# Batch 0's k and q loaded by landmark windows, with sums before the turn, in a Nystrom attention and MLP kernel on one core

## The chip, the cores and the metric

One core of a Trainium2 chip. The metric is the time on the device in microseconds (us) of one run of the kernel. TensorE (PE; its weight loads stand apart as PEld) does matrix products, VectorE (DVE) and ScalarE (ACT) the elementwise work and reductions, GpSimd (POOL) some elementwise work and DMA issues, SyncE (SP) issues most DMAs.

## The reference

Nystrom attention over 4 batches, 8 heads, 576 tokens and 64 dimensions, and two MLPs after it. The landmarks are means over windows of 18 tokens:

```python
q_lm = q.reshape(B, H, 32, 18, D).mean(axis=3)
k_lm = k.reshape(B, H, 32, 18, D).mean(axis=3)
A, Bm, C = sm(q, k_lm), sm(q_lm, k_lm), sm(q_lm, k)
Z = Bm.T / (norm1(Bm) * norminf(Bm) + 1e-6)
for _ in range(6):
    Z = 2 * Z - Z @ Bm @ Z
x = A @ Z @ C @ v
h = x @ w_in
x = (max(h, 0) + alpha * min(h, 0)) @ w_out
h = x @ w_in2
out = (h * clip(h + 3, 0, 6) / 6) @ w_out2
```

`sm` is a softmax of the scaled products. q and k have factor 8 on their draw. x is put as 2304 rows of 512 ahead of the MLPs. The MLP weights w_in, w_out, w_in2 and w_out2 come in 64-bit floats and are decoded on the chip to 32-bit.

## The kernel before, in words

Constants: P = 128 partitions, M = 32 landmarks a head, W = 18 tokens a landmark, HS = 288 (half the tokens), NF = 4 full tiles of 128 tokens and a tail of 64 tokens, NP = 4 pairs of heads, NG = 2 heads in a pair. A head h is 2 j + g.

The kernel is one long program. Batch 0's attention is the head of it: nothing of the MLP can start without it. Then the first MLP runs in 16 items for each of two blocks of tokens in each batch (`Block1`, L807 and L836: item n computes one 128-row piece of h, then adds its product with w_out). The attention of the next batch runs beside the blocks as background work, in steps. The second MLP follows at the end.

In the head (L763 to L786) the order on TensorE, VectorE, ScalarE and SP is the order of the program, written out by hand; in the blocks that holds for TensorE and SP, and a scheduler at compile time puts the others in order. Where TensorE would wait, `warm(n)` (L764) issues n idle matmuls of 512 columns; eight open the program.

Batch 0, `attention(0, ..., lat=0)`:

- `load_long` (L251): the tail of 64 tokens with tokens on partitions, and the other 512 tokens with 4 consecutive tokens of a head on a partition, for k and q in four parts of two heads each. So 5 DMAs for each of k and q, all on SP; then alpha, v in 2 DMAs, and the weights w_in and w_out.
- `transposed_long` (L294): turns k, then q, to 64 dimensions x 2 heads on the partitions and tokens in the row (kT, qT). The tail takes 4 transposes (L299); each pair of heads takes 8 matmuls with the identity (L307), each of which the profile shows as two instructions. ScalarE copies from PSUM (L300, L311) and VectorE then sums each 18 tokens of the copy to a landmark (L312). POOL copies k's landmarks into a block diagonal form `bdk` (L337), which was set to zero at the start (L153).
- `compared` (L354): products of q's landmarks with kT and with k's landmarks, for both halves of the tokens and g (L359). Then maxima on VectorE, exponentials on ScalarE (`exp_b`, `exp_c`), then `blocks`, `turned_c` (C turned, L477), `norms` (L405), `turned_rest` (L483) and `product` with v (L494).
- `scores` (L428) of tiles 0 and 1: q against k's landmarks, with bdk as moving operand (L435). Their products stand beside the softmax, their maximum ahead of the inverse and the rest inside it.
- `inverse` (L503): six steps, each a set of 8 small products (L510), then VectorE and ScalarE work. A list `fill` puts between the steps what else is to be done: a number n stands for n pieces of weight decoding (`early`, on ScalarE; `joins` brings VectorE's part), a0, n0 and t0 for steps of scores, normalisation and turning of tiles 0 and 1. A piece of w_in is two ScalarE operations on 256 columns (L202, L210) and one VectorE operation (L217); a piece of w_out has one on ScalarE (L202, 512 columns), one on POOL (L206) and one on VectorE.
- Then `project` (L698) multiplies the result with w_in's first columns, and the blocks begin. The scores of tiles 2 to 4 (a list `rest`) run in batch 0's first items.

In the blocks, item n first decodes weights up to a level that depends on how many pieces `early` did in the head (`emitted`, `LEAD`): `LEAD = max(2, emitted[0] + 1)`, where emitted[0] counts w_out pieces.

Of the kernel before, what the change touches and what calls it, by code (L numbers as in the profile page):

```python
# [64 lines left out]
def kernel(  # L65
# [28 lines left out]
    P = 128  # L94
# [15 lines left out]
    NC = FF // 512  # L110
    wide = w_in.dtype not in (F32,)
# [41 lines left out]
    nc.gpsimd.memset(bdk, 0.0)  # L153

# [96 lines left out]
    def load_long(src, b, nm, parts=1, home=None):  # L251

        if home is None:
            raw = sb.tile([P, NTI * H * D], F32, tag="raw", name=nm, bufs=2)
            home = raw[:, :NF * H * D], raw[:, NF * H * D:]
        full = home[0].rearrange("p (h c) -> p h c", h=H)
        tail = home[1][:TAIL].rearrange("p (h d) -> p h d", h=H)
        nc.sync.dma_start(out=tail, in_=src[b, :, FULL:, :].rearrange("h p d -> p h d"))
        for i in range(parts):
            hs = slice(i * H // parts, (i + 1) * H // parts)  # L260
            nc.sync.dma_start(out=full[:, hs], in_=src[b, hs, :FULL, :].rearrange("h (p t) d -> p h (t d)", t=NF))
        return full, tail

    def attention(b, bank, lat, early=None, joins=None, rest=None, warm=lambda n: None, consts=None):
# [29 lines left out]
        def transposed_long(raw, xt, lm):  # L294

            full, tail = raw
            ps = bank("tp").rearrange("q (j p) -> q j p", j=NP)
            for j in range(NP):
                nc.tensor.transpose(ps[:, j, :TAIL], tail[:, NG * j:NG * j + NG, :], ident[:TAIL, :TAIL])  # L299
            nc.scalar.copy(xt[:, :, FULL:S], ps[:, :, :TAIL])  # L300
            warm(1)
            yield True
            for j in range(NP):
                ps = bank("tp")
                for t in range(NF):
                    for g in range(NG):
                        nc.tensor.matmul(  # L307
                            ps[64 * g:64 * g + 64, t:FULL:NF], lhsT=full[:, NG * j + g, t * D:(t + 1) * D], rhs=ident,
                            start=True, stop=True,
                        )  # L310
                nc.scalar.copy(xt[:, j, :FULL], ps)  # L311
                nc.vector.tensor_reduce(  # L312
                    out=lm[:, j], in_=xt[:, j, :S].rearrange("p (l r) -> p l r", r=W), op=ALU.add, axis=AX.X
                )
                yield True

        if not lat:
            raws["k", b] = load_long(k, b, "rk", NP)
# [4 lines left out]
        qlm = small([NP, M], "qlm")  # L323
        rq = load(q, b, "rq") if lat else load_long(q, b, "rq", NP)
        turn = transposed if lat else transposed_long
# [5 lines left out]
        for _ in turn(raws["k", b], kT, kT[:, :, S:]):  # L331
            yield True
        if lat:
            rv, rv_rest = load_long(v, b, "rv")
        for g in range(NG):
            gp = slice(64 * g, 64 * g + 64)
            nc.gpsimd.tensor_copy(bdk[gp, :, g], kT[gp, :, S:])  # L337
        yield True
        for _ in turn(rq, qT, qlm):
            yield True  # L340
# [13 lines left out]
        def compared(g, hf):  # L354
            lo, hi = ((0, HS), (HS, S + M))[hf]
            ps = scs[g, hf] = bank("sc")
            for j in range(NP):
# [70 lines left out]
        def scores(tiles):  # L428
# [3 lines left out]
            for t in tiles:  # L432
                o = ps[:n, (t - t0) * 2 * P:(t - t0 + 1) * 2 * P].rearrange("p (g j l) -> p g j l", g=NG, j=NP)
                for j in range(NP):
                    nc.tensor.matmul(o[:, :, j], lhsT=qT[:, j, t * P:t * P + n], rhs=bdk[:, j], start=True, stop=True)  # L435
# [22 lines left out]
        def turned(tiles):  # L458
# [3 lines left out]
            for g in range(NG):  # L462
                for t in tiles:
                    c = (t - t0) * P
                    nc.tensor.transpose(ps[:, g, c:c + sizes[t]], es[:sizes[t], t, g], ident[:sizes[t], :sizes[t]])
# [6 lines left out]
        def turned_c(g, copy=nc.scalar.copy):  # L472
# [3 lines left out]
            for t in range(NF):  # L476
                nc.tensor.transpose(ps[:, t], pcs[:, g, t:FULL:NF], ident)  # L477
            copy(cts[0][:, g, :NF], ps)

        def turned_rest():  # L480
            ps = bank("ctp").rearrange("p (g c) -> p g c", g=NG)
            for g in range(NG):
                nc.tensor.transpose(ps[:TAIL, g, :P], pcs[:, g, FULL:], ident)  # L483
# [19 lines left out]
        def inverse():  # L503
            x = x0
            for it in range(6):
# [7 lines left out]
                if it == 5:  # L513
                    r6, vd = small([NG, P], "r6"), small([NG, D], "vd")
                    rs6 = small([NG, M], "rs6")
# [42 lines left out]
        if not lat:  # L558

            for hf in (1, 0):  # L560
                for g in range(NG):
# [6 lines left out]
            for g in range(NG):  # L568
# [9 lines left out]
            turned_rest()  # L578
            c_scale()
            drain(product())  # L580
            consts()
            warm(6)
            next(a0)
            early(1)
            n0, t0 = normalised([0, 1]), turned([0, 1])
            early(1)
            joins(1)
            fill = [[2, a0], [2, 1], [2, n0], [1, n0], [2, 1], [t0, 1], [1]]
            for i, _ in enumerate(inverse()):
# [6 lines left out]
                warm((5, 5, 4, 4, 3, 3, 6)[i])  # L596
# [166 lines left out]
    with tc.manual_schedule(engines=set(first)):  # L763
# [8 lines left out]
        warm(8)  # L772
# [492 lines left out]
```

## Time and profile before

| what | value |
|---|---|
| median of 3 runs | 810.71 us (810.41 to 810.74) |
| the profiled execution's own time | 808.85 us |
| its span in the profile | 807.0 us |
| instructions | 16974 |
| PE busy | 789.3 us (98%) |
| PEld busy | 734.3 us (91%) |
| DVE busy | 588.2 us (73%) |
| ACT busy | 455.4 us (56%) |
| POOL busy | 215.2 us (27%) |

The profile is of one execution on the chip. A busy TensorE in it is not TensorE at its peak: matmuls are pipelined and their ends are modelled, so that a matmul that is short of data can look long. The chain of waits is followed back from the last instruction: at each step to what released it, or to the instruction before it on its engine; "issue" is time in which the engine waited for nothing that the profile shows. An arrow reads as "output <- inputs", and 128x512 is partitions by elements.

### The profile page before, as it was taken

The numbers are of one execution on the slowest core, as the hardware profiler recorded it, in microseconds if no ns is written. First come the engines' busy times: TensorE is split into PE (matmuls) and PEld (weight loads), VectorE is DVE, ScalarE is ACT, GpSimd is POOL, SyncE is SP. The second block draws the span as 40 slices with busy tenths as digits, with TensorE's granted clock in tenths as the row PEclk, the third lists the DMA queues.
The fourth block names the chain that finished last, engine by engine and source line by source line (L and its number), as shares of the span: only waits on it lengthen the run. The fifth ranks groups of instructions, "written<-read, shape, count | busy, mean of one in ns | idle before, by whom it ended". The sixth has DMA issues, their size and how long they took to land.

```text
span 807.0 us, 16974 instructions
## 1 busy us (share of the span) xinstructions
PE 789.3 (98%) x6439; PEld 734.3 (91%) x6439; DVE 588.2 (73%) x1198; ACT 455.4 (56%) x987; POOL 215.2 (27%) x291
## 2 busy tenths in 40 slices
PE   9898998999999999999999999999999999999997
PEld 5476897888989989899999999999999999999997
DVE  4797776678856779566895587994677994677962
ACT  4785455676556676566773455752455741555541
POOL 0555003253423533344650232000223000322000
PEclk9999999999999999999999999999999999999999
DMA  9999006777386974369645777777867687677761
GB/s 270 408 414 287 19 32 178 276 228 232 108 246 216 311 229 141 125 205 346 216 156 195 296 267 293 269 281 254 319 231 276 257 300 247 248 268 269 259 229 59
DMA packets 90529, 190.91 MB, mean 237 GB/s; under 512 B 37184, under 2 KB 64336, under 8 KB 83792
## 3 DMA queue, kind: packets, MB, share of 16 engines
q1 hardware_dynamic: 80912, 151.55, 54.9%
q0 software_dynamic: 9536, 38.28, 13.4%
q8 instruction: 51, 0.84, 0.4%
q14 instruction: 30, 0.25, 0.1%
HBM read 146.81 MB, written 42.99 MB: 235 GB/s over the span
## 4 chain that ended last, share of the span: by engine, by line
PE 87%; DVE 5%; ACT 3%; DMA 2%; issue 1%; SPq 0%; DVEq 0%; ACTq 0%
PE acc L134 21%; PE l L134 20%; PE qa L1090 15%; PE h L134 12%; PE qb L1090 7%; PE acc L845 2%; PE wp L698 2%; PE tp L283 2%; PE sa L435 2%; PE sc L359 1%; PE psr L510 1%; DMA raw<-in_moe_w_in_dram 1%; DMA yr<-y_d 1%; ACT raw L202 1%; DMA rk<-in_k_dram 1%
## 5 line engine op out<-in xcount | busy, mean ns | idle before, releaser
L134 PE MATMUL acc<-gs,wout 128*128 128x288 f32 (+1 forms) x1344 | 205.4, 299 | 0.0
L134 PEld LDWEIGHTS acc<-gs,wout 128*128 128x128 f32 x1344 | 186.0, 188 | 3.1 <-issue 1.3
L134 PE MATMUL l<-yf,st 128*128 128x384 f32 x1008 | 175.5, 336 | 0.1
L134 PEld LDWEIGHTS l<-yf,st 128*128 128x128 f32 x1008 | 174.6, 188 | 0.5 <-DVE g L1037 0.5
L1090 PE MATMUL qa<-st,s 128*128 128x256 f32 x1008 | 147.3, 282 | 0.0
L1090 PEld LDWEIGHTS qa<-st,s 128*128 128x128 f32 x1008 | 132.1, 191 | 0.0
L134 PE MATMUL h<-a,w 128*128 128x288 f32 (+2 forms) x768 | 129.6, 304 | 1.7 <-DVE t L827 1.1
L128 ACT CAST s<-g 128x384 fp32r<-128x384 f32 x168 | 84.4, 512 | 79.1 <-PE qb L1090 51.2
L134 PEld LDWEIGHTS h<-a,w 128*128 128x128 f32 x768 | 108.5, 188 | 19.3 <-issue 4.4
L129 DVE TENSOR_TENSOR s<-g,s 128x384 fp32r<-128x384 f32 x168 | 88.9, 555 | 19.3 <-ACT s L128 16.4
L904 POOL TENSOR_TENSOR raw<-raw 128x128 f32<-128x128 f32 x128 | 73.6, 587 | 85.3 <-DMA raw<-in_moe_w_in_dram 34.8
L1051 POOL TENSOR_TENSOR p<-p,p 128x384 f32<-128x384 f32 x24 | 26.5, 1105 | 235.9 <-ACT p L1046 235.9
L1090 PE MATMUL qb<-st,s 128*128 128x256 f32 x504 | 87.4, 282 | 0.0
L827 DVE SCALAR_TENSOR_TENSOR t<-t,beta,h 128x288 f32<-128x288 f32 (+1 forms) x112 | 57.7, 515 | 34.7 <-ACT t L826 34.0
L826 ACT ACTIVATE t<-h 128x288 f32<-128x288 f32 (+2 forms) x120 | 49.6, 414 | 58.8 <-PE h L134 57.9
L1090 PEld LDWEIGHTS qb<-st,s 128*128 128x128 f32 x504 | 72.0, 191 | 0.0
L129 DVE TENSOR_TENSOR gs<-t,gs 128x288 fp32r<-128x288 f32 (+1 forms) x112 | 56.0, 500 | 19.8 <-ACT gs L128 19.5
L128 ACT CAST gs<-t 128x288 fp32r<-128x288 f32 (+1 forms) x112 | 48.9, 437 | 27.9 <-DVE t L827 26.5
L908 POOL DMA_DIRECT2D w_d<-fb x32 | 21.2, 661 | 66.9 <-DVE fb L129 37.7
L206 POOL TENSOR_SCALAR raw<-raw 128x512 int32<-128x512 uint32 x16 | 29.5, 1842 | 26.9 <-DMA raw<-in_moe_w_out_dram 26.0
L1036 ACT ACTIVATE ta<-l,three 128x384 f32<-128x384 f32 x24 | 14.0, 582 | 38.4 <-PE l L134 35.2
L845 PE MATMUL acc<-gs,raw 128*128 128x256 f32 x128 | 31.7, 385 | 0.0
(206 smaller groups left out, 1034.8 us busy)
## 6 DMA issues: line engine op xcount, KB each, us to landing
st<-w_d SPq DMA_DIRECT2D x48, 896.0 KB, 6.0
st<-w_d SPq DMA_DIRECT2D x42, 1024.0 KB, 5.9
w_d<-fb POOLq DMA_DIRECT2D x32, 512.0 KB, 4.1
w_d<-fa POOLq DMA_DIRECT2D x32, 384.0 KB, 3.3
raw<-in_moe_w_in_dram SPq DMA_DIRECT2D x16, 512.0 KB, 10.7
raw<-in_moe_w_out_dram SPq DMA_DIRECT2D x16, 512.0 KB, 11.3
raw<-in_moe_w_in_dram SPq DMA_DIRECT2D x64, 128.0 KB, 4.8
raw<-in_moe_w_out_dram SPq DMA_DIRECT2D x64, 128.0 KB, 4.6
```

The source lines that it names most:

```text
L128: nc.scalar.copy(hi, src),
L129: rest.tensor_tensor(out=lo, in0=src, in1=hi.bitcast(F32), op=ALU.subtract),
L134: nc.tensor.matmul(ps, lhsT=lhs(x), rhs=rhs(y), start=first and i == 0, stop=last and i == 2, **kw)
L206: nc.gpsimd.tensor_scalar(out=low, in0=low.bitcast(U32), scalar1=0.9374 * 2.0 ** -29, scalar2=None, op0=ALU.mult)
L283: nc.tensor.transpose(ps[:, j, :n], raw[:n, t, j * P:(j + 1) * P], ident[:n, :n])
L826: nc.scalar.activation(out=t, in_=h, func=AF.Relu, scale=-1.0),
L827: nc.vector.scalar_tensor_tensor(out=gs[:, 0] if plain else t, in0=t, scalar=beta[:, kk:kk + 1], in1=h, op0=ALU.mult, op1=ALU.add),
L845: nc.tensor.matmul(acc, lhsT=words[kk][:, ms], rhs=gs[:, 0], start=at_ == 0, stop=at_ == NK - 1)
L904: nc.gpsimd.tensor_tensor(out=y[:, o], in0=p, in1=q_, op=op)
L908: nc.gpsimd.dma_start(out=to, in_=f.bitcast(F32))
L1051: nc.gpsimd.tensor_tensor(out=p7, in0=p7, in1=p5, op=ALU.add)
L1090: nc.tensor.matmul(to[t], lhsT=s[:, y, t * P:(t + 1) * P], rhs=w[:, kp % 4, :, z], start=kp == 0 and m == 0 and t != 1, stop=kp == NU - 1 ...
```

## The change

For batch 0, k and q are loaded with the 18 tokens of a landmark on one partition (4 heads x 32 landmarks on the 128 partitions, two DMAs each). VectorE sums the 18 tokens in that layout (`summed`), and matmuls with the identity turn the sums to both halves of the partitions (`turned_sums`). One transpose turns two consecutive tokens (128 columns), so that even tokens come to lie on partitions 0 to 63 and odd tokens on 64 to 127 (`turned_run`, `placed`). The comparison, the scores, the turning of C and v's tail follow that order. The scores of tiles 0 and 1 move from beside the softmax into the inverse; the second half of q is turned after the softmax, ahead of the product with v, and placed by VectorE. bdk's memset moves to batch 1. The numbers of idle matmuls and of decoding pieces in the head change. The buffer rs6 shares one with eb.

```diff
     bdk = const.tile([P, NP, NG, M], F32, name="bdk")
-    nc.gpsimd.memset(bdk, 0.0)
...
+    def load_windows(src, b, nm):
+
+        raw = sb.tile([P, NTI * H * D], F32, tag="raw", name=nm, bufs=2)
+        x = raw[:, :2 * W * D].rearrange("p (i c) -> p i c", i=2)
+        for i in range(2):
+            nc.sync.dma_start(out=x[:, i], in_=src[b, 4 * i:4 * i + 4].rearrange("h (l r) d -> (h l) (r d)", r=W))
+        return x, raw[:, 2 * W * D:].rearrange("p (h l) -> p h l", h=H)
...
-        nc.sync.dma_start(out=tail, in_=src[b, :, FULL:, :].rearrange("h p d -> p h d"))
-        for i in range(parts):
...
+            for a in range(2):
+                nc.sync.dma_start(
+                    out=tail[a * M:(a + 1) * M], in_=src[b, :, FULL:, :].rearrange("h (c a) d -> a c h d", a=2)[a]
+                )
...
-        def transposed_long(raw, xt, lm):
...
+        def half(a):
+            return slice(HP * a, HP * a + HP)
+
+        def turned_run(raw, i, x, ps):
+            for r in range(3):
+                c = (3 * x + r) * P
+                nc.tensor.transpose(ps[:, r:3 * P:3], raw[:, i, c:c + P], ident)
+            return ps
+
+        def placed(xt, i, x, ps, copy):
+            to = xt[:, 4 * i:4 * i + 4].rearrange("q h (l r) -> q h l r", r=RR)[:, :, :, 3 * x:3 * x + 3]
+            copy(to, ps[:, :3 * P].rearrange("q (h l r) -> q h l r", h=4, r=3))
+
+        def summed(raw, i, lm):
+            nc.vector.tensor_reduce(
+                out=lm[:, 0, i * D:(i + 1) * D], in_=raw[:, i].rearrange("p (r d) -> p d r", r=W), op=ALU.add, axis=AX.X
+            )
+
+        def turned_sums(ps, i, lm):
+            for a in range(2):
+                nc.tensor.matmul(
+                    ps[half(a), i * P:(i + 1) * P], lhsT=lm[:, 0, i * D:(i + 1) * D], rhs=ident, start=True, stop=True
+                )
...
+            lms = [sb.tile([P, NG, D + 2 * M], F32, tag="nx", name="lm", bufs=2) for _ in range(2)]
+            kps = []
+            for i in range(2):
+                kps += [(i, x, turned_run(rk, i, x, bank("tp"))) for x in range(3)]
+                summed(rk, i, lms[0])
+            for i, x, ps in kps[:3]:
+                placed(kT, i, x, ps, nc.scalar.copy)
+            lk = bank("lm")
+            for i in range(2):
+                turned_sums(lk, i, lms[0])
+                summed(rq, i, lms[1])
+            for i, x, ps in kps[3:]:
+                placed(kT, i, x, ps, nc.scalar.copy)
+            nc.scalar.copy(klm, lk[:, :H * M].rearrange("p (h l) -> p h l", h=H))
+            lq = bank("lm")
+            turned_sums(lq, 0, lms[1])
+            q0 = [turned_run(rq, 0, x, (two, two, bank)[x]("tp")) for x in range(3)]
+            turned_sums(lq, 1, lms[1])
+            nc.scalar.copy(qlm, lq[:, :H * M].rearrange("p (h l) -> p h l", h=H))
...
+            if b == 1:
+                nc.gpsimd.memset(bdk, 0.0)
...
+                for x, cs in ((kT, slice(0, HS)), (klm, slice(HS, HS + M)))[:hf + 1]:
+                    for j in range(NP):
+                        h = NG * j + g
+                        nc.tensor.matmul(
+                            ps[j * M:(j + 1) * M, cs], lhsT=qlm[half(hf), h], rhs=x[half(hf), h], start=True, stop=True
+                        )
...
+                    for g in range(NG):
+                        for a in range(2):
+                            nc.tensor.matmul(
+                                o[a * n // 2:(a + 1) * n // 2, g, j], lhsT=qT[half(a), NG * j + g, t * HP:t * HP + n // 2],
+                                rhs=klm[half(a), NG * j + g], start=True, stop=True,
+                            )
...
-            for hf in (1, 0):
-                for g in range(NG):
+            for g in range(NG):
+                for hf in range(2):
                     compared(g, hf)
-            a0 = scores([0, 1])
-            next(a0)
-            most_b(range(NG))
+            for x in range(2):
+                placed(qT, 0, x, q0[x], nc.scalar.copy)
             for g in range(NG):
+                most_c(g, 0)
+                most_b([g])
+                most_c(g, 1)
+                bias_c(g)
                 exp_b(g)
-            for g in range(NG):
-                most_c(g, 1)
-                most_c(g, 0)
-                bias_c(g)
                 exp_c(g)
             blocks()
-            warm(3)
+            warm(2)
             turned_c(0)
             norms()
             turned_c(1, nc.vector.tensor_copy)
             turned_rest()
+            placed(qT, 0, 2, q0[2], nc.scalar.copy)
             c_scale()
+            q1 = [turned_run(rq, 1, x, (two, two, bank)[x]("tp")) for x in range(3)]
             drain(product())
+            for x in range(3):
+                placed(qT, 1, x, q1[x], nc.vector.tensor_copy)
             consts()
-            warm(6)
-            next(a0)
             early(1)
+            a0 = scores([0, 1])
             n0, t0 = normalised([0, 1]), turned([0, 1])
             early(1)
             joins(1)
-            fill = [[2, a0], [2, 1], [2, n0], [1, n0], [2, 1], [t0, 1], [1]]
+            fill = [[2, 1], [a0, 2], [a0, 1, a0], [1, n0], [n0, 1], [t0, 1], [1]]
...
-                warm((5, 5, 4, 4, 3, 3, 6)[i])
+                warm((3, 4, 2, 4, 3, 3, 6)[i])
...
-        warm(8)
+        warm(7)
```

## Rows read from the trace of the kernel before

**Rows 1.** The page's chain that ended last: shares of the span by engine.

```profile
PE 87%; DVE 5%; ACT 3%; DMA 2%; issue 1%; SPq 0%; DVEq 0%; ACTq 0%
```

**Rows 2.** Windows: stretch and its length, busy by engine, PEclk, DMA share, GB/s.

```profile
4.60:14.30 9.70, 9.38 (x141) 7.93 (x142) 4.76 (x7) 4.75 (x9) 0.58 (x2) 1.00 1.09 258
...
25.40:37.50 12.10, 10.96 (x135) 4.87 (x134) 8.88 (x27) 10.81 (x36) 7.48 (x5) 1.00 1.02 405
...
41.10:49.90 8.80, 7.89 (x55) 5.84 (x56) 8.02 (x15) 8.79 (x18) 6.14 (x4) 1.00 1.02 415
49.90:67.40 17.50, 15.80 (x108) 12.88 (x107) 17.30 (x42) 13.22 (x27) 11.29 (x8) 1.00 1.07 387
...
100.00:110.00 10.00, 10.00 (x75) 9.57 (x75) 8.58 (x18) 5.34 (x13) 1.47 (x2) 1.00 0.15 53
```

**Rows 3.** Chain in order of time, the head: start, us, what.

```profile
3.20 5.57 DMA rk<-in_k_dram
...
10.62 3.71 PE tp L307 x64
...
14.97 0.77 DVE qlm L312
...
15.78 1.31 PE sc L359 x19
...
22.95 0.90 PE pu L494 x40
...
24.01 1.40 PE idle L767 x6
25.41 0.51 PE psr L510 x16
...
37.60 0.81 PE wp L698 x16
```

**Rows 4.** Chain in order of time, the first block and its background work.

```profile
41.75 3.39 ACT raw L202 x6
...
49.93 0.79 DVE w L129 x2
...
67.45 0.31 PE atp L465 x2
...
69.69 0.44 PE tp L283 x4
```

**Rows 5.** Groups by form, 0 to 42 us: count, busy us, mean ns, idle before.

```profile
L312 DVE TENSOR_REDUCE qlm<-qT 128x32 f32<-128x576 f32 x4 | 3.0, 753 | 1.4 <-ACT qT L311 1.1
L311 ACT COPY qT<-tp 128x512 f32<-128x512 f32 x4 | 2.3, 587 | 1.8 <-PE tp L307 1.8
...
L435 PE MATMUL sa<-bdk,qT 128*128 128x64 f32 x16 | 2.0, 278 | 0.0
...
L478 DVE COPY ct<-ctp 128x512 f32<-128x512 f32 x1 | 0.7, 692 | 0.0
...
L300 ACT COPY qT<-tp 128x256 f32<-128x256 f32 x1 | 0.4, 378 | 0.0
...
L150 DVE TENSOR_REDUCE istack<-ident 128x32 f32<-128x128 f32 x1 | 0.4, 371 | 0.0
```

**Rows 6.** Timeline: start, us, engine, line, what; idle before in brackets.

```profile
1.15 3.59 PE L767 MATMUL idle<-idle 128*128 128x512 bf16 x8 [1.15 <-DVE idle L157]
...
1.53 2.14 SPq L261 DMA_DIRECT2D rk<-in_k_dram  x4
...
26.99 0.53 PE L510 MATMUL psr<-nx 32*32 32x96 f32 x16
...
29.23 0.53 PE L510 MATMUL psr<-nx 32*32 32x96 f32 x16 [0.53 <-DVE nx L540]
...
72.91 1.20 DVE L287 TENSOR_REDUCE kT<-kT 128x56 f32<-128x1008 f32 x1 [0.53 <-ACT kT L284]
```

**Rows 7.** Windows, the first bytes of k; columns as in rows 2.

```profile
2.00:3.00 1.00, 1.00 (x4) 0.43 (x3) 0.00 (x0) 0.01 (x1) 0.00 (x0) 1.00 0.67 144
```

More of the change, by code (lines that the diff above doesn't have):

```diff
@@ L110 @@
     NC = FF // 512
+    HP = P // 2
+    RR = W // 2
     wide = w_in.dtype not in (F32,)
@@ L292, in transposed @@
                 yield True
-        def transposed_long(raw, xt, lm):
[L296 to L305, printed above, removed]
-                    for g in range(NG):
[L307 to L313, printed above, removed]
+        def half(a):
[16 more added lines that the diff above has]
+                    ps[half(a), i * P:(i + 1) * P], lhsT=lm[:, 0, i * D:(i + 1) * D], rhs=ident, start=True, stop=True
                 )
-                yield True
         if not lat:
-            raws["k", b] = load_long(k, b, "rk", NP)
+            rk, qlm = load_windows(k, b, "rk")
         elif ("k", b) not in raws:
@@ L322, in attention @@
         qT = sb.tile([P, NP, S], F32, tag="qT", name="qT")
-        qlm = small([NP, M], "qlm")
-        rq = load(q, b, "rq") if lat else load_long(q, b, "rq", NP)
-        turn = transposed if lat else transposed_long
+        if lat:
+            qlm, rq = small([NP, M], "qlm"), load(q, b, "rq")
+        else:
+            rq, _ = load_windows(q, b, "rq")
+            klm = bdk.rearrange("p j g l -> p (j g) l")
+            kT = kT.rearrange("p j s -> p (j s)")[:, :H * HS].rearrange("p (h c) -> p h c", h=H)
+            qT = qT.rearrange("p j s -> p (j s)").rearrange("p (h c) -> p h c", h=H)
         yield True
@@ L434, in scores @@
                 for j in range(NP):
-                    nc.tensor.matmul(o[:, :, j], lhsT=qT[:, j, t * P:t * P + n], rhs=bdk[:, j], start=True, stop=True)
+                    if lat:
+                        nc.tensor.matmul(
+                            o[:, :, j], lhsT=qT[:, j, t * P:t * P + n], rhs=bdk[:, j], start=True, stop=True
+                        )
+                        continue
+                    for g in range(NG):
+                        for a in range(2):
+                            nc.tensor.matmul(
+                                o[a * n // 2:(a + 1) * n // 2, g, j], lhsT=qT[half(a), NG * j + g, t * HP:t * HP + n // 2],
+                                rhs=klm[half(a), NG * j + g], start=True, stop=True,
+                            )
             sv = ps[:n, :nh * M].rearrange("p (h l) -> p h l", l=M)
@@ L463, in turned @@
                 for t in tiles:
-                    c = (t - t0) * P
-                    nc.tensor.transpose(ps[:, g, c:c + sizes[t]], es[:sizes[t], t, g], ident[:sizes[t], :sizes[t]])
+                    to = ps[:, g, (t - t0) * P:(t - t0) * P + sizes[t]]
+                    if not lat:
+                        to = to.rearrange("p (c a) -> p a c", a=2)
+                    nc.tensor.transpose(to, es[:sizes[t], t, g], ident[:sizes[t], :sizes[t]])
             ts = slice(t0 * P, t0 * P + n)
@@ L482, in turned_rest @@
             for g in range(NG):
-                nc.tensor.transpose(ps[:TAIL, g, :P], pcs[:, g, FULL:], ident)
+                if lat:
+                    nc.tensor.transpose(ps[:TAIL, g, :P], pcs[:, g, FULL:], ident)
+                    continue
+                for a in range(2):
+                    cs = slice(a * HS + FULL // 2, (a + 1) * HS)
+                    nc.tensor.matmul(ps[a * M:(a + 1) * M, g, :P], lhsT=pcs[:, g, cs], rhs=ident, start=True, stop=True)
             nc.scalar.copy(cts[0][:TAIL, :, NF], ps[:TAIL, :, :P])
```

34 lines of the change are left out of this document (19 added, 15 removed).

## The prediction

> **What bounds the kernel now.** I read the page's chain first: TensorE carries 87% of it [rows 1], so outside the head the kernel is a row of matmuls. The windows say where it is not [rows 2]: at 100 us TensorE is full, while before 68 us each stretch has its own limit. The change edits only batch 0's attention, the head. So the question is how much earlier the full part begins; a shift there should last to the end, since all that follows is ordered against the matmuls, and the DMA engines have drained by then (share 0.15).
>
> The chain of the head [rows 3] has four pieces. (a) k's last part lands at 8.77 us; then the turns of k and q run back to back on TensorE, and q's last landmark sum ends at 15.74. (b) From 15.78 to 25.41: scores of the landmarks, softmax, turning of C, product with v, and six idle matmuls (1.40 us) ahead of the first step of the inverse. (c) From 25.41 to 37.60: the inverse, beside which ScalarE decodes w_in; ScalarE is busy 10.81 of 12.10 us, the weight loads of TensorE only 4.87 [rows 2]. (d) From 37.60 the first block starts, and the chain runs on ScalarE from 41.75 (busy 8.79 of 8.80) and on VectorE from 49.93 (17.30 of 17.50), which decode the weights [rows 2, 4]. Only the matmul at 67.45 hands it to TensorE.
>
> **Piece a.** k and q each lose 4 transposes and 64 matmul instructions; q's 64 took 3.71 us [rows 3]. In their place stand 18 transposes of 128x128 for each; four in a row take 0.44 us [rows 4], so 18 take 2.0. Turning the sums takes two pairs of products per tensor, shaped as the removed ones (a pair 0.23). The eight reductions behind ScalarE's copies (0.753 us each [rows 5]) become four that read the loaded tile and wait for the DMA alone. So the turns leave the path; what decides is the landing of q's second half and VectorE's sum after it.
>
> Landing: SP issues 4 transfers for k and q instead of 10 (2.14 us for four old ones [rows 6]); alpha's, v's (one more, for its tail) and w_in's issues behind them move up. Each new transfer is 590 KB in rows of 4.6 KB. Bytes flow from about 2.2 us (144 GB/s in that microsecond [rows 7]). The rate has two ends: 258 GB/s, what the old k, q and v got, and 415, what the stretch of 4 KB weight rows got [rows 2]. That lands 2.36 MB at 7.9 to 11.3 us, plus an estimated 0.7 for the receipt. I take the upper rate, the rows being alike in size, less a slow start: halves at about 4.5, 6.1, 7.7 and 9.2 us.
>
> Sum: 1152 elements. The two contiguous reductions, 576 in 0.753 [rows 5] and 1008 in 1.20 [rows 6], put 1.35 us on it. But the new one steps 256 bytes from element to element. The one strided reduction in the trace steps 128 bytes: 128 elements in 0.371 us [rows 5], where the contiguous line gives 0.29. If that excess goes by the element (0.66 ns), a sum costs 2.1 us; if by the instruction, 1.43. I take 1.4, as the row nearest in size and group length (18) has no excess; 2.1 is a rival below. [...]
>
> So q's last sum ends at 10.6, its turning at 10.9, a 256-column copy (0.378 [rows 5]) at 11.3, and the comparison starts at 11.35 instead of 15.78: **4.4 us earlier**. ScalarE's 6 placing copies of 384 columns a tensor (about 0.48, between 0.378 and 0.587 [rows 5]) fall at 5 to 8 us for k, ahead of that. POOL's memset and two copies for bdk, all it does from 4.6 to 14.3 us [rows 2], leave batch 0: 0.
>
> **Piece b.** The comparison has the same 16 products and 8 short ones of 32 columns; the softmax has the same operations, in the order of g. Two placing copies of q (1.0 us) stand on ScalarE ahead of its exponentials, while VectorE finds the first maxima: 0. The 16 score instructions (2.0 us [rows 5]) stood beside the softmax, so taking them from there saves nothing. Nine transposes of q (1.0 us) now stand ahead of the product, which waited for VectorE's copy until 22.95 anyway; about 0.5 us of them shows. The VectorE copies that place q's second half (0.53 each by 0.692 for 512 columns [rows 5]) end before the inverse needs VectorE. Against that the six idle matmuls go; of their 1.40 us I count 0.9, the rest being cover for ScalarE's scaling. Net **0.4 us less**.
>
> **Piece c.** The scores of tiles 0 and 1 move into the inverse, between its second and third step, as 64 instructions with 64x64 weights instead of 16 with 128x128. The ends are 22 ns an instruction (product with v, 40 in 0.90 us [rows 3]: 1.4 us) and 58 ns (the old turn: 3.7 us). The halves a=0 and a=1 use different rows and columns of the array, which favours the lower end: I take 27 ns, 1.7 us. With the step's own 0.53 and four idle matmuls (0.85) the third step comes 3.1 us after the second instead of 2.24 (26.99 to 29.23 [rows 6]). Further, VectorE's maximum and subtraction of these scores (512 elements each, like the 0.692) stand ahead of a later step. Three decoding pieces fewer (2.0 us of ScalarE) don't repay it, since ScalarE then waits for TensorE and VectorE. I put the inverse at 13.6 us instead of 12.2: **+1.4** (0.6 to 3.4).
>
> **Piece d.** The three pieces fall into the block's start, on the engine that is the chain there: ScalarE has 0.66 x 3 us more of w_in against one w_out step (0.6) less, +1.4 at most, and 0.5 if waits around the project take some. I take **+1.0**. The later scores (96 instructions for 24 before) fit into TensorE's gaps, 1.7 us between 49.9 and 67.4 [rows 2]. w_in and w_out start about 2.5 us earlier, as k, q and v are through sooner; the chain names no transfer between 8.77 and 67.45, so I cost their landing at 0.
>
> Sum: 4.4 + 0.4 - 1.4 - 1.0 = 2.4 us less. The profiled execution took 808.85 us, 1.85 more than its span of 807.0; the median of the runs is 810.71, and from there the forecast is 808.3 (806.7 to 810.0 by the ends of c and d and 0.7 us on the landing).
>
> **The rivals.** *Sums at 2.1 us*: four in a row from 4.5 us end at 12.9, the comparison starts at 13.75, and VectorE, not the DMA, sets it. The gain falls by 2.4: 810.7, no change (809.7 to 811.3). The strided row speaks for it; that its groups have 4 elements, not 18, against.
>
> *More than forecast*: what ScalarE and VectorE do from 25 to 67 us hardly changes in total and starts 4.8 us earlier. If the deferred pieces run in today's gaps (VectorE idle 3.2 of 12.1 us in c [rows 2]), c and d cost 0.5 in place of 2.4: 806.4.
>
> *The clock falls, and it gets slower.* [...] From 4.6 to 14.3 us TensorE was busy 9.38 of 9.70 [rows 2]. In the new head it has 27 transposes (3.0) and the sums' turns (0.9) between 4.2 and 11.3, with pauses up to 1.2 us. [...] For it speaks the thinner work; against it, that no pause in the trace shows a fall. [...]
>
> **How the numbers follow.** Forecast 0.48, sums at 2.1 0.22, more 0.15, the clock 0.15. Under 0.2% (1.6 us) a change can't be told from none: the forecast lies beyond it in about four of five of its cases (0.38), "more" wholly: faster 0.53. Same: 0.10 + 0.19 = 0.29. Slower: 0.15 + 0.03 = 0.18. The range 806.3 to 811.6 holds the first three and leaves out the clock and the tails.
>
> **What would show it.** Right: the comparison starts near 11.4 us, behind a q sum of 1.4; the first step of the inverse near 20.6; the project near 34.2; the hand-over at 67.45 near 65. Wrong: a strided sum over 1.9 us; idle matmuls 0.43 apart beyond 5 us; the third step over 3.5 us after the second; a new wait of TensorE for w_in in the block's start; or deferred pieces that cost nothing.

## The result, and the profile after

The changed kernel took 815.70 us in the median of six runs (814.81 to 817.96) against 810.73 for the one before: ratio 1.0059, interval 1.0041 to 1.0076. It is slower by about 5 us, where 2.4 us less was forecast. The profiled execution took 814.81 us with a span of 812.7, 5.7 more than before's 807.0.

First the page's chain by engine, as [rows 1]:

```profile
PE 89%; DVE 4%; ACT 3%; DMA 2%; issue 1%; SPq 0%; DVEq 0%; ACTq 0%
```

Then the chain in order of time (start, us, what), which answers to [rows 3, 4]:

```profile
0.73 3.86 DMA rk<-in_k_dram
...
4.61 6.26 DVE lm L320 x3
...
11.70 2.11 PE tp L312 x9
13.82 0.58 PE lm L326 x4
...
14.84 0.73 PE sc L399 x12
...
24.40 0.55 PE psr L574 x11
24.96 0.81 issue
...
27.61 1.99 PE sa L488 x64
29.60 0.97 PE idle L833 x4
...
40.00 0.81 PE wp L764 x16
...
71.68 0.31 PE atp L523 x2
```

The head now hangs on VectorE's sums (4.61), not on k's and q's turns. The comparison stands at 14.84, 0.94 earlier than before; the first inverse step is still 0.94 earlier; but the project at 40.00 is 2.4 later and the hand-over at 71.68 is 4.2 later. (The first step is taken from the timelines, 24.40 against 25.34.) All gained in the head is lost in the inverse, and more behind it.

The windows of the head (columns as in [rows 2]) show what happened to TensorE's clock:

```profile
5.00:8.00 3.00, 2.46 (x22) 1.82 (x19) 3.00 (x2) 2.73 (x6) 0.00 (x0) 1.00 1.03 415
8.00:9.00 1.00, 0.09 (x2) 0.09 (x4) 1.00 (x2) 0.06 (x1) 0.00 (x0) 1.00 1.16 260
9.00:10.00 1.00, 0.35 (x4) 0.11 (x4) 1.00 (x1) 0.37 (x1) 0.00 (x0) 1.00 1.08 226
10.00:11.00 1.00, 0.00 (x0) 0.02 (x1) 1.00 (x2) 0.00 (x0) 0.00 (x0) 0.87 1.08 347
11.00:12.00 1.00, 0.99 (x6) 0.67 (x7) 1.00 (x1) 0.00 (x0) 0.00 (x0) 0.50 1.09 348
13.00:14.00 1.00, 1.00 (x6) 0.67 (x6) 0.00 (x0) 0.00 (x0) 0.00 (x0) 0.50 1.00 397
```

VectorE is full to 12.9 us, when its last sum ends. TensorE waits for it, 0.44 us busy in the three from 8 to 11, and then is granted 0.50. q's nine transposes run in that stretch and took nearly twice what k's first nine did, in the timeline:

```profile
4.72 1.17 PE L312 MATMUL tp<-ident,rk 128*128 128x128 f32 x9 [0.53 <-DMA rk<-in_k_dram]
...
11.63 2.18 PE L312 MATMUL tp<-ident,rq 128*128 128x128 f32 x9
```

A second fall comes far behind the head, near 145 us:

```profile
142.00:144.00 2.00, 0.71 (x6) 0.57 (x7) 1.38 (x5) 0.54 (x1) 1.03 (x2) 0.97 0.45 178
144.00:146.00 2.00, 2.00 (x9) 2.00 (x9) 0.53 (x2) 0.43 (x2) 0.55 (x1) 0.50 0.46 182
146.00:148.00 2.00, 2.00 (x12) 2.00 (x11) 1.24 (x2) 2.00 (x6) 0.00 (x0) 0.68 0.50 197
```

The delay against before is still 4.2 at 94 us (the first comparison of batch 1, 94.25 in the chain, 90.02 in before's trace). The fall itself costs 1.5: psv, the last product of that batch's inverse, starts just ahead of it at 143.29 (139.27 in before, 4.02 apart), and the next project behind it at 150.67 (145.12, 5.55 apart). But it is not what is left at the end: soon behind it TensorE of before waits, by its chain for a transfer of w_in, and after has no such wait. The two cancel, and at the next project but one the delay is 4.11 again. First the rows of before, then that of after:

```profile
159.28 1.06 PE L134 MATMUL h<-a,w 128*128 128x288 f32 x6 [1.10 <-DVE t L827]
...
166.66 1.09 PE L698 MATMUL wp<-win,bd 64*32 64x512 f32 x16
```

```profile
170.77 1.09 PE L764 MATMUL wp<-win,bd 64*32 64x512 f32 x16
```

The rest of the 5.7 comes behind that, in steps whose causes I have not found.

The profiled execution is the mildest of the six: their mean granted clock is 0.989 to 0.996, on average 0.992, where 25 runs of before beside e1 have 0.997 to 1.000. By an estimate that takes time at 0.50 as half lost (q's nine transposes took 2.18 us in the fall, k's 1.17 at 1.00), (1 - 0.992) x 813.6 (the median span of the six) = 6.5 us of full-speed work is missing from an average run of after, and 0.9 from one of before. That bounds what the clock may cost: 5.6 us of difference, if all of it shows.

### The profile page after: what moved, and what is told of

It is laid out like the page before. It is cut to its first block, busy times and chain, and to the rows that moved or that the text cites. A ratio compares the mean times of both kernels' runs of the same rounds, so it can differ in the third digit from the quotient of the medians.

```text
span 812.7 us, 17039 instructions
## 1 busy us (share of the span) xinstructions
PE 788.1 (97%) x6482; PEld 733.7 (90%) x6482; DVE 594.4 (73%) x1198; ACT 455.6 (56%) x988; POOL 211.2 (26%) x289
## 4 chain that ended last, share of the span: by engine, by line
PE 89%; DVE 4%; ACT 3%; DMA 2%; issue 1%; SPq 0%; DVEq 0%; ACTq 0%
PE l L136 22%; PE acc L136 20%; PE qa L1156 15%; PE h L136 12%; PE qb L1156 7%; PE acc L911 3%; PE wp L764 2%; PE tp L295 2%; PE sa L482 2%; DMA raw<-in_moe_w_out_dram 1%; PE sc L405 1%; PE psr L574 1%; ACT raw L202 1%; DVE lm L320 1%; PE pu L558 1%
## 5 line engine op out<-in xcount | busy, mean ns | idle before, releaser
L206 POOL TENSOR_SCALAR raw<-raw 128x512 int32<-128x512 uint32 x16 | 26.7, 1667 | 27.3 <-DMA raw<-in_moe_w_out_dram 26.2
```

The source lines that it names most:

```text
L206: nc.gpsimd.tensor_scalar(out=low, in0=low.bitcast(U32), scalar1=0.9374 * 2.0 ** -29, scalar2=None, op0=ALU.mult)
```

## The experiments

Each was timed beside the kernel before on the same chip; before's own median beside them lies between 809.93 and 810.71, so the ratio is the column to compare. Stage starts are from each kernel's own trace, in us; the hand-over is the first turn of the third of the tiles 2 to 4, the row of [rows 4] at 67.45. The expectations of e2 and e5 call this mark the first turn of tiles 2 to 4; from e8 on that name stands for the turn of tile 2 (64.45 in before).

| kernel | comparison | first inverse step | project | hand-over | median | ratio to before, interval | mean clock of its runs |
|---|---|---|---|---|---|---|---|
| before | 15.78 | 25.34 | 37.53 | 67.45 | 810.73 | 1 | 0.999 |
| after | 14.84 | 24.40 | 39.93 | 71.68 | 815.70 | 1.0059 (1.0041 to 1.0076) | 0.992 |
| e1 clock held in the head | 13.70 | 24.79 | 39.25 | 73.97 | 815.22 | 1.0068 (1.0041 to 1.0094) | 0.994 |
| e2 thirteen pieces | 14.95 | 24.51 | 40.46 | 70.61 | 814.18 | 1.0048 (1.0029 to 1.0067) | 0.995 |
| e3 no idle matmuls behind the scores | 14.37 | 24.37 | 38.89 | 70.55 | 814.80 | 1.0049 (1.0025 to 1.0073) | 0.994 |
| e4 contiguous sums | 12.18 | 21.74 | 37.68 | 70.24 | 812.37 | 1.0019 (1.0004 to 1.0034) | 0.997 |
| e5 before, ten pieces | 15.78 | 25.34 | 37.54 | 69.12 | 811.81 | 1.0012 (1.0002 to 1.0023) | 0.999 |
| e6 q in the wait, scores back | 15.24 | 23.84 | 36.70 | 67.50 | 809.25 | 0.9981 (0.9967 to 0.9994) | 0.998 |
| e7 clock held throughout | 13.70 | 23.26 | 38.08 | 70.06 | 811.39 | 1.0011 (0.9997 to 1.0025) | 0.998 |
| e8 e6 with a shorter idle | 13.99 | 22.59 | 35.14 | 66.38 | 808.13 | 0.9965 (0.9952 to 0.9978) | 0.998 |
| e9 e7 with thirteen pieces | 13.98 | 23.54 | 39.24 | 69.51 | 812.23 | 1.0023 (1.0014 to 1.0033) | 0.997 |
| e10 e9, exponential later | 13.95 | 23.51 | 41.62 | 72.54 | 814.72 | 1.0048 (1.0034 to 1.0062) | 0.997 |
| e11 e8, sums in two steps | 13.46 | 22.06 | 34.99 | 65.43 | 808.97 | 0.9982 (0.9970 to 0.9993) | 0.998 |
| e12 e8 again | 14.04 | 22.64 | 35.20 | 66.15 | 809.34 | 0.9979 (0.9962 to 0.9995) | 0.998 |

e8 and e12 are one kernel: the marks of its two traces agree to 0.06 us up to the project and to 0.23 at the hand-over, while its times run from 806.2 to 812.9. So I compare stages by marks, and kernels by the ratio, never by one span.

**What a sum costs (e4).** It sums 18 neighbouring elements instead of the 18 tokens of one dimension: as many elements, read in order. It leaves out the right landmarks.

```diff
-                out=lm[:, 0, i * D:(i + 1) * D], in_=raw[:, i].rearrange("p (r d) -> p d r", r=W), op=ALU.add, axis=AX.X
+                out=lm[:, 0, i * D:(i + 1) * D], in_=raw[:, i].rearrange("p (d r) -> p d r", r=W), op=ALU.add, axis=AX.X
```

> The changed kernel with each sum read over 18 elements side by side instead of 18 elements 256 bytes apart; the same 1152 elements and 64 results. It leaves out the right choice of elements: the landmarks are sums of others. Theory (the step costs VectorE 0.75 us a sum, and the sums set the start of the comparison): a sum takes 1.35 us instead of 2.1, the last ends at about 10.3 instead of 12.9, the clock has no pause to fall in, the comparison starts at 11.0 to 11.5 instead of 14.8, and the inverse and the block follow 3 us earlier: 812 to 813. Rival (behind the comparison another limit takes over, such as v or w_in landing, or ScalarE's decoding): the comparison is 3 us earlier, the project less than 1 us, and the time stays at 815 or so.

Groups by form (count, busy us, mean ns, idle before), first of after, then of e4:

```profile
L320 DVE TENSOR_REDUCE lm<-rk 128x64 f32<-128x1152 f32 x2 | 4.2, 2164 | 2.7 <-DMA rk<-in_k_dram 2.7
L320 DVE TENSOR_REDUCE lm<-rq 128x64 f32<-128x1152 f32 x2 | 4.1, 2106 | 0.0
```

```profile
L320 DVE TENSOR_REDUCE lm<-rk 128x64 f32<-128x1152 f32 x2 | 2.7, 1353 | 2.7 <-DMA rk<-in_k_dram 2.6
L320 DVE TENSOR_REDUCE lm<-rq 128x64 f32<-128x1152 f32 x2 | 2.7, 1352 | 1.2 <-DMA rq<-in_q_dram 1.2
```

The step between elements alone takes a sum from 1.35 to 2.11 us, 0.66 ns an element. After's sums of q have no idle before them: they follow k's back to back and end at 12.9. In e4 each of q's waits for its transfer. The comparison comes 2.66 us earlier, and the clock did not fall in this head; it fell at 26.4 to 29.8, in the inverse, and again at 70.8 to 74.2. The time, 812.37, is as expected, and still no gain over before.

**The clock (e1, e7, e3).** e1 fills TensorE's waits between the turns of sums with idle matmuls; e7 adds more of them in the softmax.

```diff
+                if i:
+                    warm(5)
                 turned_sums(lk, i, lms[0])
                 summed(rq, i, lms[1])
+            warm(7)
```

> The changed kernel with 12 idle matmuls of 512 columns added where TensorE waits for the sums (5 between the two turns of k's sums, 7 behind them). [...]

With the waits filled the level stayed 1.00 up to 18 us, q's nine transposes took 1.20 us, and the comparison came at 13.70, 1.14 earlier than in after. The gain was gone by the first inverse step: the clock fell later, at 18.5, beside the softmax.

```profile
16.00:18.00 2.00, 1.01 (x4) 0.63 (x4) 1.60 (x9) 2.00 (x10) 0.00 (x0) 1.00 1.03 408
18.00:20.00 2.00, 1.46 (x6) 1.25 (x6) 0.98 (x5) 0.76 (x3) 0.00 (x0) 0.64 1.02 406
20.00:22.00 2.00, 2.00 (x14) 1.47 (x14) 1.37 (x7) 0.79 (x2) 0.00 (x0) 0.51 1.02 408
```

There the score instructions of tiles 0 and 1 used to stand (16 in 2.0 us [rows 5]); without them TensorE was busy 1.01 of the 2 us ahead of the fall. But in after's trace it is busy 1.08 of these 2 us, and the level stays 1.00 there, so that the missing scores make such a fall possible and not certain. Another fall came at 56 to 63. So e1 alone could not say what holding the clock is worth. e7 fills both places:

```diff
             blocks()
-            warm(2)
+            warm(8)
             turned_c(0)
+            warm(4)
             norms()
```

> The run with idle matmuls in the wait for the sums, and more of them beside the softmax (8 instead of 2 ahead of the first turn of C, 4 behind it), where the moved scores used to stand. Theory (in that run the clock fell beside the softmax because the scores had left): the granted clock is 1.00 up to 25 us, the comparison starts at 13.7, the first step of the inverse at 23.0 to 23.6 instead of 24.4 and 24.8, the project at 38.2 to 39. Rival (the clock falls for another reason): a stretch at 0.50 remains before 25 us.

The trace shows 1.00 throughout:

```profile
core 0: 809.9 us, clock 1.000
```

The first inverse step is at 23.26, 1.14 earlier than after, the hand-over 1.62 earlier; the ratio goes from 1.0059 to 1.0011. By the ratios, holding the clock is worth 3.9 us, 2 to 6 by their intervals. At 1.00 the project, 38.08, is still 0.55 later than before's and the hand-over 2.61 later, so something is left in the inverse and in the block's start. Why the time is only 0.9 us longer by the ratio with this mark 2.6 late, the runs don't show. e3 takes out the four idle matmuls between the scores and the third step:

```diff
-                warm((3, 4, 2, 4, 3, 3, 6)[i])
+                warm((3, 0, 2, 4, 3, 3, 6)[i])
```

> The changed kernel without the four idle matmuls behind the moved scores, between the second and third step of the inverse. Theory (TensorE's own work between these steps, 2.0 us of scores and 1.0 of idle matmuls, sets the third step): it starts 0.8 us earlier (2.6 to 2.7 us after the second instead of 3.46), and the project 0.5 to 0.8 us earlier than 40.0; the time follows within what the clock does. Rival (ScalarE's six decoding operations set it): the third step stays at 3.3 to 3.5 us after the second.

The third step came 2.56 after the second instead of 3.46, and the project 1.04 earlier; but the clock, which had stayed up in after's inverse, fell at 28.9 to 32.4, and the time is no better. The idle matmuls had a price and a use. The times of e3's nine executions go with the clock, with nothing edited between them: the one with the highest mean clock, 0.998, took 811.90 us, the one with the lowest, 0.989, 817.83.

**The deferred pieces (e2, e5, e9).** e2 puts the three decoding pieces back into after's inverse, e5 takes three out of before's.

```diff
-            fill = [[2, 1], [a0, 2], [a0, 1, a0], [1, n0], [n0, 1], [t0, 1], [1]]
+            fill = [[2, 1], [a0, 2], [a0, 1, a0, 1], [2, n0], [n0, 2], [t0, 1], [1]]
```

```diff
-            fill = [[2, a0], [2, 1], [2, n0], [1, n0], [2, 1], [t0, 1], [1]]
+            fill = [[2, a0], [2], [1, n0], [1, n0], [1, 1], [t0, 1], [1]]
```

> The changed kernel with the three decoding pieces put back into the inverse (13 instead of 10, as before the change), in its later steps, where ScalarE is idle half of the time. Theory (the three pieces lengthen the block's start, which ScalarE sets): the project starts 0 to 0.5 us later than 40.0, the first turn of tiles 2 to 4 (71.7 us) comes 1.0 to 1.8 us earlier, and the time falls by that. Rival (the block's start is set by VectorE or by the landing of w_in, so the pieces cost the same wherever they are): the turn stays within 0.5 us of 71.7 and the time within 0.5 us.

> The kernel before with three decoding pieces fewer in the inverse (10 instead of 13), and nothing else. Theory (pieces put off into the block's start are paid there): the inverse gets up to 1 us shorter, the first turn of tiles 2 to 4 (67.45) nevertheless comes 0.5 to 1.5 us later, and the time rises by as much, to 811.3 to 812.2. Rival (ScalarE's total is all that counts): what the inverse gains the block gives back, and the time stays within 0.4 us of the kernel before.

In before, whose inverse has no moved scores, the deferral changes nothing up to the project (37.54) and puts the hand-over 1.67 later, the median 1.1. In e2 the project is 0.53 later and the hand-over 1.07 earlier; the times of e2 and after can't be told apart. e9 puts the same pieces into e7, by the edit of e2:

> The changed kernel with the clock held through compare and decomposition, and all thirteen decoding pieces in the inverse. Theory (losses add up: clock, inverse, deferral): project at 38.1 to 38.6, first turn of tiles 2 to 4 at 66.0 to 66.5 instead of 67.08, the time 809.9 to 810.6, which is no change from before: the inverse's 2 us more are left, and eat the compare's gain. Rival (the deferral costs nothing once the clock is held): that turn at 67.0 to 67.2 and 811.2 to 811.6.

Both readings missed: the turn of tile 2 comes at 66.79, the time is 812.23. Against e7 the hand-over is 0.55 earlier, but the project is 1.16 later, at 39.24, and the ratio is no lower (1.0023; the intervals overlap). Its profiled execution also shows a fall of the clock, at 139 to 142.4. With the moved scores in it, the inverse gets longer by the pieces put back, here and in e2.

**Why the inverse is long (e10).** ScalarE's timeline of after between the fourth step (31.69) and the fifth (34.30):

```profile
31.54 0.42 ACT L210 ACTIVATE raw<-raw 128x256 int32<-128x256 uint32 x1
33.20 0.63 ACT L500 ACTIVATE epc<-epc 128x512 f32<-128x512 f32 x1 [1.23 <-DVE epc L499]
33.73 0.20 ACT L603 COPY nx<-psr 128x64 f32<-128x64 f32 x1
```

The step's copy of psr stands behind the scores' exponential, which waits 1.23 us for VectorE's subtraction, itself behind the maximum and a decoding piece. In before the same stretch is this:

```profile
32.10 0.20 ACT L539 COPY nx<-psr 128x64 f32<-128x64 f32 x1
```

It comes 0.82 behind its step (31.28), in after 2.04. e10 sets the exponential one step later in e9, and the normalisation later by as much:

```diff
             nc.vector.tensor_tensor(out=e, in0=sv, in1=ma.unsqueeze(2).broadcast_to([n, nh, M]), op=ALU.subtract)
+            if not lat and t0 == 0:
+                yield True
             nc.scalar.activation(out=e, in_=e, func=AF.Exp, scale=c1)
...
-            fill = [[2, 1], [a0, 2], [a0, 1, a0, 1], [2, n0], [n0, 2], [t0, 1], [1]]
+            fill = [[2, 1], [a0, 2], [a0, 1, a0, 1], [a0, 2], [n0, 2], [n0, t0, 1], [1]]
```

> As the kernel with the clock held and thirteen pieces, with the exponential of the first two tiles' scores one inverse step later than their subtraction, and their normalisation later by as much. Theory: the fifth inverse step comes 2.6 after the fourth in the changed kernel, because ScalarE waits 1.23 for VectorE's subtraction with that step's copy queued behind the exponential; with the exponential a step later that distance is 1.3 to 1.6, the project comes at 36.9 to 37.5 and the time is 809.0 to 809.9. Rival (VectorE's own work between the steps sets the distance): it stays at 2.4 to 2.6 or moves to the next step, the project stays at 38.1 to 38.6 and the time at 809.9 to 810.6.

The fifth step came 2.07 after the fourth, against 3.61 in e9: the wait in the queue was real, though 2.07 lies between the two readings (1.3 to 1.6 and 2.4 to 2.6). The total got worse, because now the last turn of these scores is late and stands ahead of the inverse's last products. TensorE's timeline of e10:

```profile
37.10 1.11 PE L528 MATMUL atp<-ident,epc 128*128 128x128 f32 x4 [2.45 <-DVE epc L516]
38.00 1.49 PE L839 MATMUL idle<-idle 128*128 128x512 bf16 x3
39.42 0.70 PE L615 MATMUL psv<-r,vd 128*64 128x128 f32 x4
```

It waits 2.45 us for VectorE, the clock falls to 0.50 behind that wait (37.0 to 40.4), and psv is 1.95 later than in e9. The scores' own softmax now ends behind the last step of the inverse (34.11).

**A version that beats both (e6, e8, e11, e12).** e6 keeps the new load, sums and turns, but turns all of q on TensorE while VectorE sums, places it by ScalarE then, and puts the scores back beside the softmax, with the pieces and idle counts of before.

```diff
+            for i, x, ps in kps[3:]:
+                placed(kT, i, x, ps, nc.scalar.copy)
+            q0 = [turned_run(rq, 0, x, bank("tp")) for x in range(3)]
             for i in range(2):
                 turned_sums(lk, i, lms[0])
                 summed(rq, i, lms[1])
...
+            q1 = [turned_run(rq, 1, x, bank("tp")) for x in range(3)]
+            for x in range(3):
+                placed(qT, 1, x, q1[x], nc.scalar.copy)
             lq = bank("lm")
+            warm(2)
             turned_sums(lq, 0, lms[1])
+            warm(8)
             turned_sums(lq, 1, lms[1])
...
+            a0 = scores([0, 1])
+            next(a0)
             for g in range(NG):
                 most_c(g, 0)
...
-            fill = [[2, 1], [a0, 2], [a0, 1, a0], [1, n0], [n0, 1], [t0, 1], [1]]
+            fill = [[2, a0], [2, 1], [2, n0], [1, n0], [2, 1], [t0, 1], [1]]
```

> A version: loads and sums as in the changed kernel, but all of q is turned and placed while the sums run (TensorE and ScalarE are idle there), idle matmuls hold the clock, and the scores of tiles 0 and 1 stand beside the softmax again, with the list of 13 pieces and the idle matmuls of the kernel before in the inverse. Theory (the loss is in the moved scores, the put-off pieces and the clock, not in the loads): the granted clock is 1.00 in the head, the comparison starts at 13.7 to 13.9, the first step of the inverse at 22.3 to 23.0 instead of 25.3 before, the project at 34.5 to 35.3 instead of 37.5, and the time is 2 to 3 us under the kernel before, 807.7 to 808.8. Rival (earlier is not better: ScalarE's decoding or a transfer sets the project): the project stays at 37 or later and the time at 810 to 811.

It is faster than before by 0.2% (0.9981, the interval ends at 0.9994), between the two readings, though its marks came some 1.5 later than expected. The cause is in its timeline:

```profile
12.50 1.90 PE L837 MATMUL idle<-idle 128*128 128x512 bf16 x8
...
14.33 0.44 PE L326 MATMUL lm<-ident,lm 128*64 128x128 f32 x4
```

The last sum had ended at 12.95; its turn waited until 14.33, behind the eight idle matmuls that I had put there. e8 has two of them there in place of eight:

```diff
-            warm(8)
+            warm(2)
             turned_sums(lq, 1, lms[1])
```

> As the version with q turned in the wait, with two idle matmuls instead of eight ahead of the last turn of the sums. Theory: there the last four turns of landmarks stood behind eight idle matmuls until 14.33, while VectorE's last sum ended at 12.95, so the comparison came at 15.24; with two it comes at 13.9 to 14.1, and every mark up to the project is 1.1 to 1.3 earlier (first inverse step 22.6 to 22.8, project 35.4 to 35.7). What the end makes of it tells two readings apart. If the start of the block is bound by VectorE's and ScalarE's work and the weights there, the first turn of tiles 2 to 4 stays at 64.2 to 64.6 and the time is 808.9 to 809.5; if the project carries through, that turn comes at 63.2 to 63.5 and the time is 807.8 to 808.4.

The marks came as expected (13.99, 22.59) or a little earlier (35.14), and by the second reading the head carries through: the first turn of tiles 2 to 4 is at 63.38 (the hand-over 1.12 earlier than in e6), the time 808.13, the ratio 0.9965. Its inverse takes 12.55 from first step to project, as against 15.53 in after. Of the 2.39 that the project gained on before, 1.07 is left at the hand-over. The chain of e8 names transfers:

```profile
7.70 9.13 DMA raw<-in_moe_w_in_dram
...
16.85 11.33 DMA raw<-in_moe_w_out_dram
...
28.20 10.17 DMA raw<-in_moe_w_out_dram
...
38.39 12.83 DMA raw<-in_moe_w_out_dram
```

From 7.7 to 51.2 it runs over the transfers of the experts' weights, where the chain of before names no transfer between 8.77 and 67.45. I took it that they are late next, and take part of the gain. The chain of e12, the same kernel, does not bear that out. It names k's load and no transfer behind it up to 110 us:

```profile
0.72 3.93 DMA rk<-in_k_dram
```

So what holds back the rest of the 2.39 is open. e11 makes the sums cheaper, so that the head gets still earlier:

```diff
+            c = W // 2 * D
+            nc.vector.tensor_tensor(out=part, in0=raw[:, i, :c], in1=raw[:, i, c:], op=ALU.add)
             nc.vector.tensor_reduce(
-                out=lm[:, 0, i * D:(i + 1) * D], in_=raw[:, i].rearrange("p (r d) -> p d r", r=W), op=ALU.add, axis=AX.X
+                out=lm[:, 0, i * D:(i + 1) * D], in_=part.rearrange("p (r d) -> p d r", r=W // 2), op=ALU.add, axis=AX.X
             )
```

> As the version with q turned in the wait and two idle matmuls, each sum made in two instructions: the first nine tokens plus the last nine (576 elements, read in order), then the strided sum of the nine. Estimate from the runs: 0.76 for the addition (512 elements took 0.68) and 1.05 for half of the strided sum of 2.1, so 1.75 to 1.85 a sum in place of 2.1; the comparison at 12.6 to 13.1 (13.99), the project at 33.8 to 34.3 (35.14). Two readings of the time: if what follows is bound by the transfers of the experts' raw weights, which make up the chain of waits of that version from 7.7 to 51.2, the first turn of tiles 2 to 4 stays at 63.2 to 63.5 and the time at 807.8 to 808.5; if the head still carries through, that turn is at 62.3 to 62.6 and the time at 806.9 to 807.4.

> The version with q turned in the wait and two idle matmuls once more, unchanged, beside the one with sums in two steps. If its gain is a property of the kernel, the time is 807.7 to 808.9 and the ratio to before 0.995 to 0.998; if it came from the one series of runs, the ratio is above 0.998.

VectorE's timeline of e11, one sum:

```profile
4.68 0.76 DVE L321 TENSOR_TENSOR qT<-rk 128x576 f32<-128x576 f32 x1 [2.73 <-DMA rk<-in_k_dram]
5.47 1.17 DVE L322 TENSOR_REDUCE lm<-qT 128x64 f32<-128x576 f32 x1
```

1.93 a sum, not 1.8: the addition was priced right, half of a strided sum costs more than half. The comparison came 0.58 before e12's, the project 0.21, the hand-over 0.72; the times of the two (808.97 and 809.34) are one within their intervals. The mark (first turn at 62.60) fits the head that carries through, the time fits neither reading, so whether a still earlier head pays is open. e12 shows a gain again, a smaller one: its ratio, 0.9979, lies just inside the first reading, its time, 809.34, outside. All four series of this version lie below before, by 0.2 to 0.35%.

## Why the prediction was wrong

In the prediction's own terms, up to the hand-over of the profiled execution: piece a gave 0.94 of its 4.4, piece b nothing of its 0.4, piece c took 3.3 instead of 1.4 and piece d 1.8 instead of 1.0. That is 4.2 later, where 2.4 earlier was forecast.

**Piece a, the landing: right.** Halves were to land near 4.5, 6.1, 7.7 and 9.2; the first sum starts at 4.61, and in e4, whose sums of q wait for their transfers, these start at 7.91 and 9.86, 0.2 and 0.7 late. The 0.7 us for the receipt was an estimate: the last transfer of before moves no bytes behind 805.7 and lands at 806.1, some 0.4 later.

**Piece a, "I take 1.4" for a sum: the first step that failed.** It is 2.11, and the rival *Sums at 2.1* had the mechanism, the end of the sums (12.9) and the excess of 0.66 ns an element (its own rows give 0.64). I chose between the two prices by the length of the groups; the row that had the step of the addresses was the one to go by, and e4 shows what the step costs: 2.11 us with it, 1.35 without. It is not the whole miss: with sums at 1.35 the comparison of e4 comes at 12.18, not at 11.35, and the ratio is 1.0019. By the ratios the sums, with the fall that they bring, stand for some 3 of the 7.4 us between forecast and median.

**The clock: a rival that I gave 0.15, and the one that came, but not in the way that I priced.** I argued that no pause in the trace showed a fall. But I took the head's pauses for sums of 1.4. With 2.1 TensorE was idle for 2.56 of the 3 us from 8 to 11 and the level fell; with 1.35, in e4, the head kept 1.00. So that rival and this one are one event, not two: the slow sum makes the pause, the pause the fall, and the fall nearly doubles q's transposes (2.18 us against 1.17), so that the comparison came at 14.84 instead of that rival's 13.75. I had priced a low level that lasts into the inverse, an estimate that no run shows: in the profiled execution the fall ended near 14.2, ahead of the comparison, and the median of 815.7 has the losses of pieces c and d in it as well. Nor did the mark show that I had named, idle matmuls 0.43 apart beyond 5 us. That is how the first ones of before stand (their weight loads at 1.98, 2.41 and 2.83 us); those of after's head, from 16.24 on, stand 0.22 apart (2 in 0.60 us, 6 in 1.47) and none lies in the fall. What the clock cost came in other places too, beside the softmax (e1), in the inverse (e3, e4) or in the blocks; e7 is what shows its size, roughly. That rests on a change from 1.0059 to 1.0011 between kernels that differ by idle matmuls alone. Where it falls in each of after's other five runs is not seen.

Transposes alone did not bring the level down: with k's transposes it stayed 1.00 from 5 to 8 us, and fell behind the pause. In e4 transposes and turns of the sums are all that TensorE did from 4.63 to 11.71 us, and the level stayed 1.00. In e8 TensorE was busy 7.51 of the 8 us from 4 to 12, of which 5.37 are transposes and the rest turns of the sums and idle matmuls:

```profile
4.00:8.00 4.00, 3.51 (x21) 3.01 (x21) 3.35 (x2) 2.24 (x5) 0.00 (x0) 1.00 1.02 409
8.00:12.00 4.00, 4.00 (x34) 2.64 (x32) 4.00 (x3) 3.56 (x9) 0.00 (x0) 1.00 1.11 320
```

**Piece b, 0.4 less: no gain.** From comparison to first step it is 9.56 in both kernels. Of q's nine transposes ahead of the product about 0.5 was to show; in after's chain they stand in full:

```profile
21.18 1.13 PE tp L312 x9
```

In e8, which has turned all of q by then, the same stretch takes 8.60. "Taking them from there saves nothing" was true of the path and false of the clock: the scores also kept TensorE at work beside the softmax, where the level fell in e1.

**Piece c, +1.4: it was +3.3, the second step that failed**, though just inside its bounds (15.53 instead of 12.19). The scores' 64 instructions took 2.05 us (32 ns each, nearer the lower end of 22 than the 58, where I had estimated 27), so the third step came 3.46 after the second (3.1 forecast). I named VectorE's maximum and subtraction "ahead of a later step", and left some 0.5 for them and all else behind the third step: the fifth step came 2.61 after the fourth instead of 1.56, and the sixth 2.04 after that instead of 1.22. What I had not seen is ScalarE's queue, with the step's copy behind an exponential that waits for VectorE. With idle counts and pieces as in before and the scores back beside the softmax, e8's inverse takes 12.55; e9's, with the scores in it and as many pieces, 15.70, at 1.00 both. So the inverse with the scores in it is what costs; idle counts and the places of the pieces differ too, and the scores' own share is not isolated. The first step's extra 0.81 is an "issue" gap, in which the trace shows no cause; e7 has no such gap (its second step comes 2.03 after the first, after's 2.64).

**Piece d, +1.0: right in kind.** The block's start, project to hand-over, took 31.75 instead of 29.92. Three pieces account for 1.67 by e5, 1.60 by e2 (31.75 to 30.15), above the 1.4 that I called the most. Their landing at 0: right for after, whose chain names no transfer of weights up to 110 us; for the version with the faster head it is open (e8, e12).

## What to carry to other kernels

When work is taken off the path, ask what else it did: here scores that cost nothing kept TensorE busy in a stretch where its clock could then fall (to 0.51 in e1), and the place they moved to had a queue, ScalarE's, that waited for them in the program's order (1.23 us). Price a reduction by the row with its stride, not by the one with its length (2.11 us with the stride, 1.35 without). And where the longer wait of one rival is the condition of another, give them one chance together.

## What was not expected

The clock's falls are not tied to one place. In before TensorE is as thinly used near 137 us as in after ahead of its fall near 145 (0.73 of 2 us against 0.71), and stays at 1.00:

```profile
134.00:136.00 2.00, 0.88 (x19) 0.74 (x20) 2.00 (x6) 1.78 (x4) 1.92 (x4) 1.00 0.00 0
...
138.00:140.00 2.00, 0.73 (x6) 0.59 (x7) 1.38 (x5) 0.54 (x1) 1.00 (x2) 1.00 0.47 184
```

e8's profile has a fall at 139.6 to 143, e12's, the same kernel, none there but one at 66 to 70. One profiled execution can be 3 us from its kernel's median: e12's took 812.32 (median 809.34), e11's, at 1.00 throughout, 806.09 (808.97). What decides in which execution a pause brings the level down, the runs don't show.
